# The last 96 FFN columns computed token-major and transposed back by DMA, with the layer norm of the first tile put alone at the front of DVE and ACT

## The chip, the cores and the metric

The kernel runs on one core of one Trainium2 chip. The metric is device time in microseconds (us). "Timed" means runs in rounds of this kernel and the kernel before on the same chip; "the trace" is one profiled execution.

Engines: PE is TensorE (matmul), PEld its weight load, DVE is VectorE, ACT is ScalarE, POOL is GpSimd, SP issues the DMAs. PE's results arrive in the memory called PSUM; `bn_stats` and `bn_aggr` are the DVE instructions for mean and variance. N is the number of columns that a matmul streams, M the number of output partitions.

## The reference

```python
# x: (1, 2048, 512); wqkv: (512, 1536); wo: (512, 512); w1: (512, 1376); w2: (1376, 512); bf16
x = x + A(layernorm(x), wqkv, wo)       # linear attention, 32 heads, phi(t) = where(t>0, t+1, exp(t)) + 1e-6
x = x + B(layernorm(x), w1, w2)         # B: relu(x @ w1) @ w2
x = x + A(layernorm(x), wqkv, wo)
x = x + B(layernorm(x), w1, w2)
```

1376 is ten times 128 plus 96: the last group of FFN columns is not full.

## The kernel before

The kernel writes all instructions into a graph with estimated durations. A list scheduler and a random search then fix the order on each engine. Any edit to the graph makes the search start anew and may move instructions everywhere.

Tokens are handled in 16 tiles of 128, four tiles to a chunk. `Tb` holds the normalized tokens transposed, `xn` untransposed. The first chunk is transposed on PE, the others by DMA from SP. The first half of FFN, in the kernel before (cuts marked):

```python
def b_h(t):
    for c in range(NFC):                       # NFC = 11
        M = 128 if c < NFC - 1 else FLAST      # FLAST = 96
        b = alloc_bank()
        mm_group(... [(psv[0:M, b, :], w1[:, d, 128*c:128*c+M], Tb[:, 4*t:4*t+4, d, :], d == 0, d == 3, False)
                      for d in range(4)] ...)  # 4 matmuls of N=512, also for M=96
        # relu by ACT or DVE into big, columns on partitions
```

The head (first chunk), tile by tile:

```python
def ln_tile_first(i):
    if i in ACT_STATS:     # (2, 3): sum and sum of squares on ACT, small steps on DVE
        ...
    else:                  # tiles 0, 1: bn_stats and bn_aggr on DVE
        ln_stats_first(i)
    # DVE: veps = max(var, 0) + eps;  POOL: rstd = veps ** -0.5;  DVE: nbias = -mean * rstd
    ln_norm(i, True, keys=[("rstd1", i), ("nbias1", i)])   # ACT or DVE
# then, per tile: transpose_pe(i): 4 PE transposes, copied out of PSUM by ACT or DVE
```

Ahead of the head, 12 matmuls on zeros (`WARM=12`) keep PE busy while the first loads arrive.

## Time and profile before

| | before |
|---|---|
| time, median of 6 runs | 289.91 us (289.64 to 290.19) |
| traced execution, span | 288.4 us (it was timed at 290.33) |
| PE busy | 98% |
| start to start of 128x512 matmuls | 216 ns |

The page of the kernel before: busy time of each engine (part 1), and the chain of work that ended last, by engine (part 4).

```profile
PE 282.3 (98%) x1447; PEld 127.9 (44%) x1447; DVE 175.3 (61%) x482; ACT 177.7 (62%) x362; POOL 35.0 (12%) x45
...
PE 90%; DVE 4%; DMA 4%; SPq 0%; issue 0%; ACT 0%
```

PE bounds the kernel, and little else is on the path. "Busy" PE overstates that, because matmuls are pipelined (mean 379 ns each, but one starts every 216 ns). So the holes are read from start times. PE's timeline, before (start, length, engine, line, operation, output and inputs, shape, count, and in brackets the idle time before it with what ended it):

```profile
7.03 1.04 PE L672 MATMUL ps<-wqkv,Tb 128*128 128x512 bf16 x4 [0.69 <-ACT Tb L642]
...
10.61 1.89 PE L672 MATMUL ps<-wqkv,Tb 128*128 128x512 bf16 x8
12.33 1.89 PE L672 MATMUL ps<-Tb,wqkv 128*128 128x512 bf16 x8
...
24.82 1.04 PE L672 MATMUL ps<-wqkv,Tb 128*128 128x512 bf16 x4 [0.24 <-DMA Tb<-xn]
...
45.00 1.06 PE L672 MATMUL ps<-GT,wqkv 128*128 128x128 bf16 x16
...
99.98 9.66 PE L672 MATMUL ps<-Tb,w 128*128 128x512 bf16 x44
...
131.78 6.22 PE L672 MATMUL ps<-Tb,w 128*128 128x512 bf16 x28 [0.54 <-DVE big L852]
...
182.94 1.06 PE L672 MATMUL ps<-GT,wqkv 128*128 128x128 bf16 x16
```

The matmuls `ps<-wqkv,Tb` are the key projections of one tile each, `ps<-Tb,wqkv` the query projections, `ps<-Tb,w` the FFN's first half (44 of them for a chunk, at 99.98 us). The bracket counts idle time after the modelled end of the matmul before; the real loss is the start-to-start time less 216 ns. At 24.82 us (ninth key projection) the gap is 615 ns, so 0.40 us is lost; at 131.78 us it is 918 ns, so 0.70 us is lost. The matmuls on `GT` mark the middle of each attention layer; I use them as milestones, because all the same work lies ahead of them in every kernel here.

The chain of waits, before, in order of time (start, length, what):

```profile
2.23 6.26 DMA xin<-in_A_x_dram
8.50 0.02 issue
8.52 1.29 DVE bst L582 x2
...
19.60 5.17 DMA Tb<-xn
...
24.82 105.58 PE ps L672 x572
```

Until 24.8 us the chain is: second load of x (tiles 4 to 7, landing at 8.50 us; tiles 0 to 3 come ahead of it, in two pieces), work on DVE, then the third DMA transpose of `xn` (tiles 8 and 9). The transpose takes 5.17 us; the page's median for these transposes is 3.2 us.

### The profile page before, as it was taken

What the parts mean: (1) busy time and instruction counts of PE and PEld (TensorE: products, weight loads), DVE (VectorE), ACT (ScalarE), POOL (GpSimd) and SP (SyncE); (2) the same over time, 40 slices, a digit from 0 to 9 for tenths busy, and PEclk for the clock granted to TensorE, in tenths of its full rate; (3) what the DMA queues carried; (4) which work ended last, traced back from release to release, by engine and by line L of the source; (5) the groups of instructions that cost most, each with busy time, mean ns of one, the idle gap of its engine ahead of it and who ended that gap; (6) DMA issues with size and microseconds to landing.
All of it is one profiled execution on the core that took longest, in us unless ns stands there. A gap on an engine that the chain in (4) does not pass through costs nothing.

```text
span 288.4 us, 3983 instructions
## 1 busy us (share of the span) xinstructions
PE 282.3 (98%) x1447; PEld 127.9 (44%) x1447; DVE 175.3 (61%) x482; ACT 177.7 (62%) x362; POOL 35.0 (12%) x45
## 2 busy tenths in 40 slices
PE   7999999999999999999999999999999999999996
PEld 2444454444444444443444444444444444444444
DVE  5899539998358652493345786899854954130233
ACT  5997649999666483586533665999966427316000
POOL 4211000002001110050301373000110011000000
PEclk9999999999999999999999999999999999999999
DMA  7976760213003070030003120012300323001022
GB/s 225 349 101 93 218 211 0 54 22 73 0 2 73 0 146 2 1 73 0 3 0 73 34 41 0 0 35 40 75 2 0 73 71 77 0 32 43 0 73 73
DMA packets 40163, 17.22 MB, mean 60 GB/s; under 512 B 31985, under 2 KB 39633, under 8 KB 40145
## 3 DMA queue, kind: packets, MB, share of 16 engines
q1 hardware_dynamic: 40144, 16.98, 24.8%
q8 instruction: 11, 0.18, 0.3%
q14 instruction: 8, 0.06, 0.1%
HBM read 7.01 MB, written 2.10 MB: 32 GB/s over the span
## 4 chain that ended last, share of the span: by engine, by line
PE 90%; DVE 4%; DMA 4%; SPq 0%; issue 0%; ACT 0%
PE ps L672 90%; DMA xin<-in_A_x_dram 2%; DMA Tb<-xn 2%; DVE bst L582 2%; DVE xn L614 1%; DVE big L658 0%; DVE emscr L656 0%; DVE big L852 0%; DVE mv L583 0%; ACT big L851 0%; DVE xin L870 0%; SPq L539 0%; SPq L534 0%; SPq L536 0%; DVE veps L590 0%
## 5 line engine op out<-in xcount | busy, mean ns | idle before, releaser
L672 PE MATMUL ps<-Tb,w 128*128 128x512 bf16 (+1 forms) x352 | 78.5, 379 | 0.5 <-DVE big L852 0.5
L672 PE MATMUL ps<-w,big 128*128 128x512 bf16 (+2 forms) x363 | 77.3, 372 | 0.0
L851 ACT ACTIVATE big<-ps 128x512 bf16<-128x512 f32 (+1 forms) x79 | 47.0, 601 | 28.2 <-PE ps L672 27.8
L679 ACT ACTIVATE sqscr<-xres 128x512 bf16<-128x512 f32 x48 | 30.0, 626 | 39.3 <-DVE xres L716 25.9
L672 PEld LDWEIGHTS ps<-w,big 128*128 128x128 bf16 (+1 forms) x363 | 35.5, 98 | 40.8
L672 PEld LDWEIGHTS ps<-Tb,w 128*128 128x128 bf16 (+1 forms) x352 | 34.5, 100 | 41.6 <-issue 1.8
L654 ACT ACTIVATE escr<-ps 128x512 bf16<-128x512 f32 x64 | 37.8, 617 | 8.4 <-PE ps L672 8.2
L652 ACT ACTIVATE big<-ps 128x512 bf16<-128x512 f32 x64 | 38.5, 619 | 2.5 <-PE ps L672 2.5
L712 DVE SCALAR_TENSOR_TENSOR xin<-ps,rstdf,xres 128x512 bf16<-128x512 f32 x15 | 11.3, 750 | 37.6 <-PE ps L672 37.5
L672 PE MATMUL ps<-wqkv,Tb 128*128 128x512 bf16 x128 | 31.9, 379 | 1.2 <-ACT Tb L642 0.9
L672 PE MATMUL ps<-big,xn 128*128 128x512 bf16 x128 | 32.2, 379 | 0.0
L658 DVE TENSOR_TENSOR big<-big,emscr 128x512 bf16<-128x512 bf16 x64 | 30.0, 484 | 3.4 <-ACT big L652 2.1
L656 DVE TENSOR_SCALAR emscr<-escr 128x512 bf16<-128x512 bf16 x64 | 21.2, 342 | 14.6 <-ACT escr L654 14.0
L672 PE MATMUL ps<-Tb,wqkv 128*128 128x512 bf16 x128 | 30.0, 379 | 0.0
L672 PE MATMUL ps<-Wp,big 128*128 128x512 bf16 x128 | 29.3, 379 | 0.0
L716 DVE SCALAR_TENSOR_TENSOR xres<-ps,rstdf,xres 128x512 f32<-128x512 f32 x16 | 12.0, 750 | 22.3 <-PE ps L672 22.1
L705 POOL TENSOR_TENSOR rstdf<-varf,nhalf 128x4 f32<-128x4 f32 x8 | 8.3, 1042 | 132.7 <-DVE nm2f L699 75.2
L830 DVE TENSOR_TENSOR big<-big,ps 128x512 bf16<-128x512 bf16 x32 | 20.0, 681 | 3.4 <-PE ps L672 3.4
L672 PEld LDWEIGHTS ps<-wqkv,Tb 128*128 128x128 bf16 x128 | 12.1, 98 | 16.2 <-ACT Tb L642 1.6
L672 PEld LDWEIGHTS ps<-Wp,big 128*128 128x128 bf16 x128 | 12.2, 98 | 15.4 <-DVE Wp L762 0.8
L672 PEld LDWEIGHTS ps<-Tb,wqkv 128*128 128x128 bf16 x128 | 12.2, 98 | 15.0 <-DVE nmf L688 0.5
L672 PEld LDWEIGHTS ps<-big,xn 128*128 128x128 bf16 x128 | 12.2, 98 | 14.6 <-issue 0.5
(89 smaller groups left out, 201.4 us busy)
## 6 DMA issues: line engine op xcount, KB each, us to landing
wqkv<-in_A_wqkv_dram SPq DMA_DIRECT2D x3, 512.0 KB, 7.2
xin<-in_A_x_dram SPq DMA_DIRECT2D x3, 512.0 KB, 8.2
out_dram<-xin SPq DMA_DIRECT2D x3, 512.0 KB, 2.9
w<-in_B_w_dram SPq DMA_DIRECT2D x1, 1376.0 KB, 6.5
w<-in_B_w_dram SPq DMA_DIRECT2D x1, 1280.0 KB, 9.6
wo<-in_A_wo_dram SPq DMA_DIRECT2D x1, 512.0 KB, 8.8
Tb<-xn SPq DMA_TRANSPOSE x30, 3.2
xin<-in_A_x_dram SPq DMA_DIRECT2D x1, 384.0 KB, 3.0
```

The lines of the kernel that those rows point to most:

```text
L582: g.add(DVE, lambda e: e.bn_stats(bst[:, i, :], xin[:, i, :]), [("xin", i)], [("bst", i)], C_DVE_BNST, name="bnst%d" % i)
L652: g.add(ACT, lambda e: e.activation(dst_ap, psv[:, b, :], ACTF.Identity, bias=1.0 + 1e-6, scale=1.0), [("ps", b)], [dst_key], C_ACT_PSUM, ...
L654: g.add(ACT, lambda e: e.activation(escr[:, s, :], psv[:, b, :], ACTF.Exp), [("ps", b)], [("escr", s)], C_ACT_EXP, name=name + "_exp")
L656: g.add(DVE, lambda e: e.tensor_scalar(emscr[:, s, :], escr[:, s, :], 1.0, 1e-6, ALU.min, ALU.add), [("escr", s)], [("emscr", s)], C_DVE_B ...
L658: g.add(DVE, lambda e: e.tensor_tensor(dst_ap, dst_ap, emscr[:, s, :], ALU.max), [dst_key, ("emscr", s)], [dst_key], 340.0, name=name + "_ ...
L672: last = e.matmul(o, l, r, start=st, stop=sp, skip_group_check=skip)
L679: g.add(ACT, lambda e: e.activation(sqscr[:, q, :], xres[:, i, :], ACTF.Square, accum_out=dst[:, i:i + 1]), [("xres", i)], [("sqscr", q), ...
L705: g.add(POOL, lambda e: e.tensor_tensor(rstdf[:, sl], varf[:, sl], nhalf[:, 0:4], ALU.pow), [("varf", t), ("nhalf",)], [("rstdf", t)], C_P ...
L712: g.add(DVE, lambda e: e.scalar_tensor_tensor(xin[:, i, :], psv[:, b, :], rstdf[:, i:i + 1], xres[:, i, :], ALU.mult, ALU.add), rd, [("xin ...
L716: g.add(DVE, lambda e: e.scalar_tensor_tensor(xres[:, i, :], psv[:, b, :], rstdf[:, i:i + 1], xres[:, i, :], ALU.mult, ALU.add, accum_out= ...
L830: g.add(DVE, lambda e, j=j: e.tensor_tensor(unit_ap(us[j]), unit_ap(us[j]), psv[:, GB[j], :], ALU.mult), [("big", us[j]), ("ps", GB[j])], ...
L851: g.add_flex([(ACT, lambda e, M=M, b=b, u=u: e.activation(unit_ap(u, M), psv[0:M, b, :], ACTF.Relu), C_ACT_PSUM), (DVE, lambda e, M=M, b=b ...
```

## The change

The intent, as far as the diff tells it: the 96 columns use 96 of the 128 output partitions, yet cost PE as much as a full group. Computed with tokens as the output partitions, they need N=96 per matmul, so PE streams 16 x 96 columns instead of 4 x 512. The result then has tokens on partitions, so a DMA transpose turns it back. In the head, tile 0 shall be normalized as early as possible: fewer other instructions in front of it, `rstd` by ACT (`Ln`, then `Exp`) for tiles 0 and 1, two warm-up matmuls fewer.

```diff
-... WARM=12, ... SEARCH=1200, ... ACT_STATS=(2, 3)):
+... WARM=10, ... SEARCH=1500, ... ACT_STATS=(2,), REM_TOK=True, RSTD_ACT=(0, 1), FILL=(0,), HEAD_DEP=True):
+        def b_h_rem(t, c, M, b):
+            mm_group(lambda: [(psv[:, b, M*il:M*il+M], Tb[:, 4*t+il, d, :], w1[:, d, 128*c:128*c+M],
+                               d == 0, d == 3, False) for il in range(4) for d in range(4)], ...)
+            # relu of 128 x 4*96 into hrt (ACT or DVE)
+            dma(lambda e: e.dma_start_transpose(unit_ap(u)..., hrt[:, r, :, :]...), ...)
         def b_h(t):
-            for c in range(NFC):
+            for c in ([NFC - 1] + list(range(NFC - 1)) if REM_TOK else range(NFC)):
 ...
-                ln_stats_first(i)
+                ln_stats_first(i, [("xn", i - 1)] if 0 < i < 3 and HEAD_DEP else [])
-            g.add(POOL, ... rstd = veps ** -0.5 ...)      # all tiles
+            if i in RSTD_ACT:                             # tiles 0, 1
+                g.add(ACT, ... lnv = Ln(var + eps) ...); g.add(ACT, ... rstd = Exp(-0.5 * lnv) ...)
-            g.add(DVE, ... nbias = -mean * rstd ...); ln_norm(i, True, ...)        # ACT or DVE
+            g.add(DVE, ... xn = (xin - mean) * rstd ...)                           # DVE alone
```

(`FILL` adds one matmul on zeros behind the transposes of tile 0. POOL also clears `hrt` once.)

More of the change, by code (lines that the diff above doesn't have):

```diff
@@ L24 @@
 C_ACT_SQ = 620.0
+C_ACT_TINY = 220.0
 C_DVE_PSUM = 600.0
@@ L406, in build_kernel @@
 def build_kernel(nc, A_x, A_wqkv, A_wo, B_w1, B_w2, out, n_layers_pairs=2, Q_LATE=3, O_PE_CHUNKS=3, PHI_PATH=3,
-                 KV_LAG=2, INTERLEAVE=True, WARM=12, SPLIT_CHUNKS=1, TAIL_SPLIT=True,
+                 KV_LAG=2, INTERLEAVE=True, WARM=10, SPLIT_CHUNKS=1, TAIL_SPLIT=True,
                  PHI_K=3, PHI_QE=3, PHI_QL=3, LAST_HALVES=True, ZH_FIRST=True, P2_TIGHT=False,
-                 FIRST_PE_CHUNKS=1, TGK=2, TGF=2, FT_PE=0, WP_GB=True, WO_LAG=1, DEN_PRE=1, LATE_A=1, ITERS=12, BOOST=3000.0, SEARCH=1200, ZP=(0, 3), WK_ACT=False, ACT_STATS=(2, 3)):
+                 FIRST_PE_CHUNKS=1, TGK=2, TGF=2, FT_PE=0, WP_GB=True, WO_LAG=1, DEN_PRE=1, LATE_A=1, ITERS=12, BOOST=3000.0, SEARCH=1500, ZP=(0, 3), WK_ACT=False, ACT_STATS=(2,), REM_TOK=True, RSTD_ACT=(0, 1), FILL=(0,), HEAD_DEP=True):
     S = A_x.shape[1]
@@ L474, in build_kernel @@
         zhl = sb("zhl", [128, 2, 512], BF16)
+        hrt = sb("hrt", [128, 2, 4, 128], BF16)
+        eps5 = sb("eps5", [128, 1], F32)
+        lnv = sb("lnv", [128, NT], F32)
         GT = sb("GT", [128, 4, 512], BF16)
@@ L501, in build_kernel @@
         psv = _PS()
-        scr_state = {"e": 0, "sq": 0, "ln": 0}
+        scr_state = {"e": 0, "sq": 0, "ln": 0, "rem": 0}
         def dma(emit, reads, writes, xfer_ns, name, eng=SP, issue=C_SP_ISSUE):
@@ L568, in build_kernel @@
         g.add(POOL, lambda e: e.memset(eps6[:], 1e-6), [], [("eps6",)], 100, name="ms_eps6")
+        g.add(POOL, lambda e: e.memset(eps5[:], EPS), [], [("eps5",)], 100, name="ms_eps5")
         g.add(POOL, lambda e: e.memset(ones[:], 1.0), [], [("ones",)], 200, name="ms_onesb")
@@ L579, in build_kernel, with ln_stats_first @@
               [("m1f",)], [("bmask",)], 300, name="as3")
-        def ln_stats_first(i):
-            g.add(DVE, lambda e: e.bn_stats(bst[:, i, :], xin[:, i, :]), [("xin", i)], [("bst", i)], C_DVE_BNST, name="bnst%d" % i)
+        if REM_TOK:
+            g.add(POOL, lambda e: e.memset(hrt[:], 0.0), [], [("hrt0",), ("hrt", 0), ("hrt", 1)], 400, name="ms_hrt")
+        def ln_stats_first(i, behind=()):
+            g.add(DVE, lambda e: e.bn_stats(bst[:, i, :], xin[:, i, :]), [("xin", i)] + list(behind), [("bst", i)], C_DVE_BNST, name="bnst%d" % i)
             g.add(DVE, lambda e: e.bn_aggr(mv[:, i, :], bst[:, i, :]), [("bst", i)], [("mean", i), ("var", i)], C_DVE_SMALL, name="bnag%d" % i)
@@ L605, in ln_chunk, with ln_norm @@
                   [("mean", i) for i in tl] + [("rstd", t)], [("nbias", t)], C_DVE_SMALL, name="nbias%d" % t)
-        def ln_norm(i, first, eng=None, keys=None):
+        def ln_norm(i, first, eng=None):
             t = i // 4
@@ L610, in ln_norm @@
             skey = ("xin", i) if first else ("xres", i)
-            rd = [skey] + (keys or [("rstd", t), ("nbias", t)])
+            rd = [skey, ("rstd", t), ("nbias", t)]
             alts = [(ACT, lambda e: e.activation(xn[:, i, :], src, ACTF.Identity, scale=rstd[:, i:i + 1], bias=nbias[:, i:i + 1]),
@@ L627, in tr_chunk, with transpose_pe @@
                 tr_dma(lo, lo + grain)
-        def transpose_pe(i):
+        def transpose_pe(i, fill=False):
             b = alloc_bank()
@@ L639, in _emit @@
                 return last
-            g.add(PE, _emit, [("xn", i), ("ident",)], [("ps", b)], 4 * C_MM128, name="trp%d" % i)
+            g.add(PE, _emit, [("xn", i), ("ident",)], [("ps", b)] + ([("fill", i)] if fill else []), 4 * C_MM128, name="trp%d" % i)
+            if fill:
+                g.add(PE, lambda e: e.matmul(psv[:, wt, :], wrm[:, 0:128], wrm[:, :], start=True, stop=True),
+                      [("fill", i)], [("ps", wt)], C_MM512, name="fill%d" % i)
             dst = Tb[:, i, :, :].rearrange("p c t -> p (c t)")
@@ L841, in build_kernel, with src @@
         hcount = [0]
+        def b_h_rem(t, c, M, b):
+            r = scr_state["rem"]
+            scr_state["rem"] = (r + 1) % 2
+            mm_group(lambda: [(psv[:, b, M * il:M * il + M], Tb[:, 4 * t + il, d, :], w1[:, d, 128 * c:128 * c + M],
+                               d == 0, d == 3, False) for il in range(4) for d in range(4)],
+                     [("T", i) for i in range(4 * t, 4 * t + 4)] + [("w1",)], [("ps", b)], 16 * (M / 2.4 + 2.5), "hr%d" % t)
+            def src():
+                return psv[:, b, 0:4 * M].rearrange("p (i m) -> p i m", m=M)
+            g.add_flex([(ACT, lambda e: e.activation(hrt[:, r, :, 0:M], src(), ACTF.Relu), C_ACT_PSUM - 80.0),
+                        (DVE, lambda e: e.tensor_scalar(hrt[:, r, :, 0:M], src(), 0.0, None, ALU.max), C_DVE_FLEX - 120.0)],
+                       [("ps", b), ("hrt0",)], [("hrt", r)], name="hrr%d" % t)
+            u = h_unit(c, t)
+            dma(lambda e: e.dma_start_transpose(unit_ap(u).rearrange("p (i t) -> p i t", t=128),
+                                                hrt[:, r, :, :].rearrange("p i m -> p (i m)")),
+                [("hrt", r)], [("big", u)], 2200.0, "hrt%d" % t, issue=C_SP_TR)
         def b_h(t):
-            for c in range(NFC):
+            for c in ([NFC - 1] + list(range(NFC - 1)) if REM_TOK else range(NFC)):
                 M = 128 if c < NFC - 1 else FLAST
                 b = alloc_bank()
+                if REM_TOK and M < 128:
+                    b_h_rem(t, c, M, b)
+                    continue
                 mm_group(lambda b=b, c=c, M=M: [(psv[0:M, b, :], w1[:, d, 128 * c:128 * c + M], Tb[:, 4 * t:4 * t + 4, d, :],
@@ L911, in ln_tile_first @@
                 g.add(ACT, lambda e: e.activation(sqscr[:, 0, :], xin[:, i, :], ACTF.Identity, accum_out=s1[:, c]),
-                      [("xin", i)], [("sqscr", 0), ("s1", i)], C_ACT_SQ, name="sm%d" % i)
+                      [("xin", i), ("rstd1", 0)], [("sqscr", 0), ("s1", i)], C_ACT_SQ, name="sm%d" % i)
                 g.add(ACT, lambda e: e.activation(sqscr[:, 1, :], xin[:, i, :], ACTF.Square, accum_out=s2[:, c]),
@@ L921, in ln_tile_first @@
             else:
-                ln_stats_first(i)
-            g.add(DVE, lambda e: e.tensor_scalar(veps[:, c], mv[:, i, 1:2], 0.0, EPS, ALU.max, ALU.add),
-                  [("var", i)], [("veps1", i)], C_DVE_SMALL, name="veps%d" % i)
-            g.add(POOL, lambda e: e.tensor_tensor(rstd[:, c], veps[:, c], nhalf[:, 0:1], ALU.pow),
-                  [("veps1", i), ("nhalf",)], [("rstd1", i)], C_POOL_POW1, name="rstd%d" % i)
-            g.add(DVE, lambda e: e.scalar_tensor_tensor(nbias[:, c], mv[:, i, 0:1], -1.0, rstd[:, c], ALU.mult, ALU.mult),
-                  [("mean", i), ("rstd1", i)], [("nbias1", i)], C_DVE_SMALL, name="nbias%d" % i)
-            ln_norm(i, True, keys=[("rstd1", i), ("nbias1", i)])
+                ln_stats_first(i, [("xn", i - 1)] if 0 < i < 3 and HEAD_DEP else [])
+            if i in RSTD_ACT:
+                g.add(ACT, lambda e: e.activation(lnv[:, c], mv[:, i, 1:2], ACTF.Ln, bias=eps5[:, 0:1]),
+                      [("var", i), ("eps5",)], [("lnv", i)], C_ACT_TINY, name="lnv%d" % i)
+                g.add(ACT, lambda e: e.activation(rstd[:, c], lnv[:, c], ACTF.Exp, scale=-0.5),
+                      [("lnv", i)], [("rstd1", i)], C_ACT_TINY, name="rstd%d" % i)
+            else:
+                g.add(DVE, lambda e: e.tensor_scalar(veps[:, c], mv[:, i, 1:2], 0.0, EPS, ALU.max, ALU.add),
+                      [("var", i)], [("veps1", i)], C_DVE_SMALL, name="veps%d" % i)
+                g.add(POOL, lambda e: e.tensor_tensor(rstd[:, c], veps[:, c], nhalf[:, 0:1], ALU.pow),
+                      [("veps1", i), ("nhalf",)], [("rstd1", i)], C_POOL_POW1, name="rstd%d" % i)
+            g.add(DVE, lambda e: e.tensor_scalar(xn[:, i, :], xin[:, i, :], mv[:, i, 0:1], rstd[:, c], ALU.subtract, ALU.mult),
+                  [("xin", i), ("mean", i), ("rstd1", i)], [("xn", i)], C_DVE_NORM_BF, name="norm%d" % i)
         def ln_first(t):
@@ L936, in ln_first @@
                     if t < FIRST_PE_CHUNKS:
-                        transpose_pe(i)
+                        transpose_pe(i, i in FILL)
                     for o in g.ops[n0:]:
```

## The prediction

> **What bounds the kernel now.** TensorE. The page gives PE 98% busy at full clock, but busy time counts pipelined matmuls, so I read start-to-start times: a 128x512 matmul follows the last every 216 ns, and from 10.4 us to the end of the last group (about 285.7 us) only two holes exceed 0.35 us: 0.40 us before the matmuls at 24.82 us (waiting for the third transpose of xn, which took 5.2 us to land instead of the median 3.2) and 0.70 us before those at 131.78 us (waiting for an eviction by DVE). The chain of waits says the same: 90% matmuls. DVE (61%) and ACT (62%) have slack except in the first 25 us, where the chain runs through DVE from the landing of the second x load (8.50 us) to 19.60 us.
>
> **The FFN part.** Eight times, four matmuls of N=512 with M=96 (4 x 216 = 864 ns) become sixteen of N=96 with fresh 128x128 weights each. The sixteen 128x128 matmuls on GT at 45.0 us start every 56 ns, which fits N/2.4 + 2.5 ns in the Trainium skill, "TensorE: Matmul & The Clock Gate", section "Wait — 56ns, not 53.3ns?"; the same page's section "Back-to-back issue gap" would give about 81 ns for N=128 with weight loads, which this trace does not show. The 128x1 matmuls start every 25 ns with new weights, so weights do not bind. Estimate: 16 x 42.6 = 681 ns, a gain of 183 ns per chunk, 1.46 us in all, all on the critical path. The relu eviction shrinks (512 to 384 elements) but is off the path. The eight new DMA transposes cost the queue 1.23 us each and land in about 3.2 us; with the 96-column group first in its chunk, more than 8 us of matmuls lie before their reader. I expect no wait for them.
>
> **The head.** Two warm-up matmuls fewer frees PE at 5.48 us instead of 5.96. rstd of tile 0 goes through two small ACT instructions instead of POOL, but the instruction order puts a 0.63 us Square (waiting for the load that lands at 4.22) between them, and on DVE a bn_stats, aggregate and eps lie before the normalization. I expect tile 0 normalized at about 5.7 us (before: 5.44), transposed at 5.8 (before 5.96), first projection at 6.8 (before 7.03). That lead is not kept: DVE's order has bn_stats of tile 4, whose data lands at 8.50 us, ahead of the normalizations of tiles 1 and 2. DVE will idle about 1.2 us, tile 1 is normalized at about 9.5 us, and the fourth projection ends near 12.9 us, against 12.33. Part returns at the 24.2 us wait, which should shrink. Net estimate: +0.2 us (-0.3 to +0.6).
>
> **The wait at 131 us.** The schedule was searched anew; there ACT now evicts more of the FFN groups. I count half of the 0.7 us as gone: -0.3.
>
> **Sum.** 289.81 - 1.46 + 0.2 - 0.3 = 288.25 us; 8 in 10 between 287.4 and 289.3. Chances: faster by over 2%: 0.01; within 2%: 0.98; slower: 0.01.
>
> **What would show it.** Starts of the N=96 matmuls every 42 to 44 ns; no wait of PE for big written by the new transposes; DVE idle until about 8.5 us before a bn_stats, with tile 1 normalized after it; the first query projection starting at 12.6 to 13.0 us; first projection before 7.0 us.
>
> **What would make it wrong.** N=96 matmuls bound at 56 ns or above (no gain in the FFN); the new transposes delaying those of xn behind them in the one queue; new holes in PE where the new order meets evictions; a clock that rises later because of the shorter warm-up; the x load landing elsewhere than at 8.5 us.

## The result

| | before | changed |
|---|---|---|
| time, median of 6 runs | 289.91 us (289.64 to 290.19) | 289.26 us (288.99 to 289.65) |
| ratio | | 0.9978 (0.9965 to 0.9991) |
| traced execution, span | 288.4 us | 287.3 us |

A ratio is the mean time of one kernel's fast runs over that of the other's of the same rounds, so it is not quite the ratio of the medians. The median lies inside the predicted range, but the gain is 0.65 us where I predicted 1.56 us.

The page of the changed kernel, the same parts as before:

```profile
PE 280.5 (98%) x1542; PEld 129.5 (45%) x1542; DVE 176.0 (61%) x478; ACT 174.4 (61%) x359; POOL 34.8 (12%) x45
...
PE 94%; DMA 4%; DVE 1%; SPq 0%; ACT 0%; issue 0%
```

PE's timeline, changed, the lines that answer to those of before (and the new ones of N=96):

```profile
7.21 1.04 PE L683 MATMUL ps<-wqkv,Tb 128*128 128x512 bf16 x4 [0.47 <-ACT Tb L653]
...
9.62 0.40 PE L646 MATMUL ps<-ident,xn 128*128 128x128 bf16 x4 [1.16 <-DVE xn L964]
...
12.78 3.62 PE L683 MATMUL ps<-Tb,wqkv 128*128 128x512 bf16 x16
...
25.77 1.04 PE L683 MATMUL ps<-wqkv,Tb 128*128 128x512 bf16 x4 [0.74 <-DMA Tb<-xn]
...
45.95 1.06 PE L683 MATMUL ps<-GT,wqkv 128*128 128x128 bf16 x16
...
100.57 0.84 PE L683 MATMUL ps<-w,Tb 128*128 128x96 bf16 x16
101.25 8.80 PE L683 MATMUL ps<-Tb,w 128*128 128x512 bf16 x40
...
128.71 8.97 PE L683 MATMUL ps<-Tb,w 128*128 128x512 bf16 x40
...
182.63 1.06 PE L683 MATMUL ps<-GT,wqkv 128*128 128x128 bf16 x16
```

The sixteen matmuls of N=96 take 101.25 - 100.57 = 0.68 us; their starts lie 42.5 ns apart. The hole at 131 us is nearly gone: its group starts 380 ns after the last, so 0.17 us is lost instead of 0.70. The hole before the ninth key projection has grown: the gap is 1122 ns, so 0.90 us is lost instead of 0.40. The matmuls on `GT` start 0.95 us later.

The chain of waits, changed: again load, DVE, third transpose.

```profile
2.23 6.30 DMA xin<-in_A_x_dram
8.54 0.02 issue
8.56 0.69 DVE bst L590
...
20.49 5.24 DMA Tb<-xn
...
25.77 106.56 PE ps L683 x628
```

The third transpose takes 5.24 us again, but is issued at 20.49 us instead of 19.60. DVE's timeline, changed, shows what was put where:

```profile
7.53 0.15 DVE L960 TENSOR_SCALAR veps<-mv 128x1 f32<-128x1 f32 x1
8.56 0.69 DVE L590 BATCH_NORM_STATS2 bst<-xin 128x6 f32<-128x512 bf16 x1 [0.88 <-DMA xin<-in_A_x_dram]
9.17 0.40 DVE L964 TENSOR_SCALAR xn<-xin,mv,rstd 128x512 bf16<-128x512 bf16 x1
9.48 0.42 DVE L654 COPY Tb<-ps 128x512 bf16<-128x512 bf16 x1
9.82 0.41 DVE L964 TENSOR_SCALAR xn<-xin,mv,rstd 128x512 bf16<-128x512 bf16 x1
```

DVE idles 0.88 us for the load of tile 4. Behind it stand the normalization of tile 1 (9.17 us), the copy of tile 3 (9.48) and the normalization of tile 2 (9.82), none of which needs that load. The `rstd` of tile 1 was ready at 7.7 us. In the kernel before, DVE normalized tile 1 (or 2) at 6.70 us, and only one tile of the head stood behind the load. DVE's timeline, before:

```profile
8.52 1.29 DVE L582 BATCH_NORM_STATS2 bst<-xin 128x6 f32<-128x512 bf16 x2 [0.56 <-DMA xin<-in_A_x_dram]
...
9.90 0.41 DVE L614 TENSOR_SCALAR xn<-xin,rstd,nbias 128x512 bf16<-128x512 bf16 x1
```

The new buffer `hrt`, in the view of one tile's instructions:

```profile
L863 ACT ACTIVATE hrt<-ps x8: 469/491/586, 62.0 to 257.0; 128x384 bf16<-128x384 f32 x8
...
who waited for it (us, times):
busy tenths in 40 slices 1000000000000000000000000000000000000000
DMA to landing us min/median/max: 2.4/2.8/4.2
```

The list of who waited is empty, and the new transposes land in 2.8 us.

**The sum by stages.** Span cut at the starts of the two groups on `GT`; all from traces. The second x load lands at a different time in each execution (8.11 to 9.21 us), and in most kernels here the head shifts with it, so I also give the head counted from that landing.

| kernel (trace) | x load lands | to first GT | from the landing | first GT to second | second GT to end |
|---|---|---|---|---|---|
| before | 8.50 | 45.00 | 36.50 | 137.94 | 105.41 |
| r_before (same kernel) | 8.81 | 44.90 | 36.09 | 137.94 | 105.42 |
| changed | 8.54 | 45.95 | 37.41 | 136.68 | 104.65 |
| r_after (same kernel) | 8.31 | 45.62 | 37.31 | 136.67 | 104.67 |
| a_ffn | 8.18 | 44.27 | 36.09 | 136.72 | 104.95 |
| r_ffn (same kernel) | 8.56 | 44.69 | 36.13 | 136.72 | 104.94 |
| b_head | 8.93 | 46.04 | 37.11 | 137.47 | 105.41 |
| d2_order | 9.09 | 44.83 | 35.74 | 136.68 | 104.67 |
| r_d2 (same kernel) | 8.82 | 44.88 | 36.06 | 136.67 | 104.67 |

From GT to the end, four 96-column groups became shorter: -0.76 us. Between the two GT there are four more, and the 131 us hole: -1.26 us, of which -0.53 is the hole. So the FFN groups gave about 1.49 us and the hole 0.53. The head took back 0.9 to 1.3 us counted from the landing.

### The profile page after: what moved, and what is told of

The parts are those of the page before. It is cut to its first block, busy times and chain, and to the rows that moved or that the text cites. A ratio compares the mean times of both kernels' runs of the same rounds, so it can differ in the third digit from the quotient of the medians.

```text
span 287.3 us, 4176 instructions
## 1 busy us (share of the span) xinstructions
PE 280.5 (98%) x1542; PEld 129.5 (45%) x1542; DVE 176.0 (61%) x478; ACT 174.4 (61%) x359; POOL 34.8 (12%) x45
## 4 chain that ended last, share of the span: by engine, by line
PE 94%; DMA 4%; DVE 1%; SPq 0%; ACT 0%; issue 0%
PE ps L683 93%; DMA xin<-in_A_x_dram 2%; DMA Tb<-xn 2%; DVE bst L590 0%; PE ps L646 0%; ACT escr L665 0%; DVE xin L901 0%; SPq L543 0%; SPq L538 0%; SPq L540 0%; DVE xn L964 0%
## 5 line engine op out<-in xcount | busy, mean ns | idle before, releaser
L683 PE MATMUL ps<-Tb,w 128*128 128x512 bf16 x320 | 71.6, 379 | 0.0
L882 ACT ACTIVATE big<-ps 128x512 bf16<-128x512 f32 x69 | 41.0, 599 | 16.8 <-PE ps L683 16.4
L683 PEld LDWEIGHTS ps<-Tb,w 128*128 128x128 bf16 x320 | 30.5, 98 | 36.3 <-issue 0.9
L663 ACT ACTIVATE big<-ps 128x512 bf16<-128x512 f32 x64 | 38.2, 614 | 2.6 <-PE ps L683 2.6
```

Of the source, the lines that this page charges most:

```text
L663: g.add(ACT, lambda e: e.activation(dst_ap, psv[:, b, :], ACTF.Identity, bias=1.0 + 1e-6, scale=1.0), [("ps", b)], [dst_key], C_ACT_PSUM, ...
L683: last = e.matmul(o, l, r, start=st, stop=sp, skip_group_check=skip)
L882: g.add_flex([(ACT, lambda e, M=M, b=b, u=u: e.activation(unit_ap(u, M), psv[0:M, b, :], ACTF.Relu), C_ACT_PSUM), (DVE, lambda e, M=M, b=b ...
```

## The experiments

Two theories of the head's loss: (T1) the **order on DVE**, which puts ready work behind the load; (T2) the **instruction fetch of PE**. The packets in the trace show instructions being fetched by DMA in blocks of 16 KB on one queue. That these are PE's is inferred from their number: 11 before and 12 in the changed kernel, where PE has 2,926 and 3,123 instructions in the trace. In these two kernels one such fetch comes after 82 to 84 matmuls, at 20.43 us (before) and 21.56 us (changed), while the third transpose is in flight, and that transpose is the slow one. A rival to both: the head is neutral, and the FFN part lost its gain in new waits.

### c_fetch: the fetch moved by the warm-up's shape (orders kept)

```diff
-                for k in range(WARM):
-                    last = e.matmul(psv[:, wt, :], wrm[:, 0:128], wrm[:, :], start=True, stop=True)
+                for k in range(60):
+                    last = e.matmul(psv[:, wt, 0:80], wrm[:, 0:128], wrm[:, 0:80], start=True, stop=True)
```

> The changed kernel, with its warm-up as 60 matmuls of N=80 in place of 10 of N=512: every engine's order is otherwise the same. In both traces TensorE's 16 KB instruction fetch comes after 82 to 84 matmuls, at 20.4 us (before) and 21.6 us (changed), in the middle of the third transpose of xn, which then takes 5.2 us instead of 3.1. Theory (the fetch delays that transpose, and this is the lost part of the gain): with 50 more matmuls ahead, the fetch comes at about 11 to 13 us, the third transpose lands in 3.0 to 3.5 us, TensorE's 0.9 us hole at 24.9 us closes to under 0.1 us, and the time falls by about 0.9 us against the changed kernel, to about 288.3 us. Rival (the third transpose is slow for another reason, such as the load of the queue or of SBUF at that time): it still takes about 5.2 us, the hole stays, time 289.2 us.

Measured: 288.78 us median (287.51 to 291.27), ratio 0.9971 (0.9934 to 1.0008). The fetch came at 14.62 us, the third transpose was issued at 20.84 us and landed at 23.90, after 3.06 us, and the hole was gone. PE's timeline of c_fetch:

```profile
7.17 1.89 PE L683 MATMUL ps<-wqkv,Tb 128*128 128x512 bf16 x4 [0.69 <-ACT Tb L653]
...
25.23 1.03 PE L683 MATMUL ps<-wqkv,Tb 128*128 128x512 bf16 x4
```

But the first key projection took 1.89 us instead of 1.04 (first line), while the ninth started without a wait (last line): the granted clock rose to full only at 10.7 us (5.5 us in the changed kernel). Two of the six runs had mean clocks of 0.988 and 0.994 and took 291.1 and 291.3 us. So the run agrees with T2 about the transpose; its time is inconclusive.

### d_bn4: one instruction moved behind the normalization of tile 1 (rest kept)

```diff
         order, total = _list_schedule(...)
+        # in order[DVE]: take "bnst4" out, put it back right after "norm1"
```

> The changed kernel with one DVE instruction moved after scheduling: bn_stats of tile 4 (whose data lands at 8.5 us) goes behind the normalization of tile 1, nothing else. Theory A (the head is late because DVE's order holds tile 1 behind that load, and the first matmuls bound everything after): tile 1 is normalized at about 8.2 us instead of 9.6, the first query projection starts 0.3 us earlier (12.4 to 12.5 us), and the time falls by 0.3 us. Theory B (what counts is the third transpose with its delay by the instruction fetch, released by DVE's whole work after 8.5 us): DVE has one 0.33 us normalization less after 8.5 us, so the third transpose may start 0.3 us earlier, but the fetch also comes 0.3 us earlier; the hole at 24.9 us keeps about its 0.9 us. Both say 288.9 to 289.0 us; they differ in the hole: 0.9 us if it moves with the rest, 1.2 us (and no gain at all) if the transpose does not move.

Measured: 288.90 us, ratio 0.9965 (0.9951 to 0.9980). In its trace tile 1 was normalized at 7.57 us, but the next instruction behind the load was now the copy of tile 3, which PE needed first: the next key projection did not start before 10.31 us, with the load landing at 9.21 us. The hole before the ninth key projection was 0.92 us, the third transpose took 5.26 us. So the wait moved to the next victim. The run does not tell the two theories apart as I had hoped; it showed that the whole group has to move.

### a_ffn: the FFN part alone, with the old head (schedule searched anew)

```diff
 (kernel before)
+        hrt = sb("hrt", [128, 2, 4, 128], BF16)      # with its clearing by POOL, b_h_rem and the new loop in b_h
```

> The kernel before with the FFN part of the change alone (old head, 12 warm-up matmuls, old search length; the schedule is searched anew). Theory (FFN part worth 1.46 us, head part negative): each 16 matmuls of N=96 take 0.68 us, no wait of TensorE for the new transposes, head as before (fifth to eighth projections as before, hole at 24.2 us about 0.4 us), hole at 131 us anywhere in 0 to 0.7 us: time 287.9 to 288.5 us, faster than the full change. Rival (the FFN part loses some of its gain in new waits and the head is neutral): about 289.2 us.

Measured: 288.34 us, ratio 0.9948 (0.9918 to 0.9977). By the median it is faster than the full change, but one of its six runs (290.88 us at a mean clock of 0.992) widens the interval until it overlaps that of the change; r_ffn below settles it. No wait for the new transposes.

### b_head: the head part alone (schedule searched anew)

```diff
 (changed kernel)
-... REM_TOK=True, ...
+... REM_TOK=False, ...
```

> The changed kernel with the FFN part undone (96-row groups as before), new head kept, schedule searched anew. Theory (the head part costs about 0.9 us): about 290.3 to 290.9 us, slower than before, with the hole before the ninth key projection at 0.5 us or more. Rival (head neutral): 289.7 to 290.0 us.

Measured: 290.67 us, ratio 1.0022 (1.0003 to 1.0042): slower than before by 0.64 us, although its hole at 131 us shrank to 0.18 us too. That shrinking therefore comes from the search and not from the FFN part. Counted from the landing, its head is 0.6 to 1.0 us longer than before. The hole before the ninth projection was only 0.12 us, not the 0.5 that I expected: this schedule lost its time earlier, its first query projection starting at 13.53 us. The rival "FFN part lost its gain" falls with these two runs.

### c2_pad and f2_before_pad: the fetch moved by satisfied waits (orders kept)

```diff
                     last = e.matmul(psv[:, wt, :], wrm[:, 0:128], wrm[:, :], start=True, stop=True)
+                    for _w in range(10):
+                        e.wait_ge(sem_eng[DVE], 1)
```

> The changed kernel with ten already satisfied waits after each of its ten warm-up matmuls: 100 more instructions for TensorE to fetch, no other work, same orders, and (other than in c_fetch) the warm-up matmuls as they were, so the clock should rise at about 5.4 us again. Theory (TensorE's instruction fetch delays the third transpose of xn): the 16 KB fetch comes before 17 us instead of at 21.6, the third transpose takes 3.0 to 3.5 us instead of 5.2, TensorE's 0.9 us hole before the ninth key projection is under 0.1 us, the matmuls on GT start at about 45.05 us instead of 45.95, and the time is 0.9 us below the changed kernel: 288.2 to 288.6 us. Rival (the transpose is slow for another reason; c_fetch moved it by its changed clock): hole and time as in the changed kernel, 289.2 us.

Measured: 289.96 us, ratio 0.9987 (0.9963 to 1.0011). The waits were not free: warm-up matmuls started about 550 ns apart instead of 427, so the transposes of tile 0 began at 6.96 us instead of 6.12. And the fetch did not come before 17 us, but at 19.49, into the **second** transpose. That one now took 4.57 us, and the third took 3.06. PE's timeline of c2_pad has the hole at the seventh key projection:

```profile
20.48 1.03 PE L685 MATMUL ps<-big,xn 128*128 128x512 bf16 x4
22.10 1.04 PE L685 MATMUL ps<-wqkv,Tb 128*128 128x512 bf16 x4 [0.59 <-DMA Tb<-xn]
```

The hole followed the fetch from the third transpose to the second. The time says nothing, as the head was delayed otherwise.

> The kernel before with the same padding (120 more waits behind its 12 warm-up matmuls). Theory: its third transpose of xn lands in 3.0 to 3.5 us instead of 5.2, the 0.4 us hole before 24.8 us closes, the time falls by 0.4 us to about 289.5 us. Rival: no change, 290.0 us.

Measured: 291.50 us, ratio 1.0051 (1.0029 to 1.0074), slower: the first key projection started at 9.06 us instead of 7.03. The hole before the ninth projection was gone, but with PE that late it would be gone anyway. Its third transpose took 3.69 us, although no 16 KB fetch fell into it (that came at 15.87 us); a fetch of 8 KB on another queue did, at 22.74 us. A miss: the padding cost more than what it was to measure.

### d2_order: the whole group in front of the load (rest kept)

```diff
         order, total = _list_schedule(...)
+        # in order[DVE], the eight from "bnst4" to "trev2" become:
+        want = ["norm1", "trev3", "norm2", "bnst4", "bnst5", "trev2", "bnag4", "bnst6"]
```

(`norm` is a normalization, `trev` the copy of a transposed tile out of PSUM, `bnst` bn_stats, `bnag` its aggregate.)

> The changed kernel with eight DVE instructions reordered after scheduling: normalization of tile 1, the copy of the transposed tile 3, the normalization of tile 2 come ahead of the bn_stats of tile 4 (data at 8.2 to 9.2 us), and bn_stats of tiles 4 and 5 ahead of the copy of tile 2; nothing else moves. Theory: the first four key projections end about 1.0 us earlier and the first query projection starts at 11.7 to 12.0 us instead of 12.8; but the fetch still falls on the third transpose, so the hole before the ninth key projection grows to about 1 to 1.5 us, and the matmuls on GT start only 0.3 to 0.7 us earlier: 288.6 to 289.0 us. Rival (order of DVE in the head is what costs, the fetch is a bystander): the whole 1.0 us arrives at the end, 288.2 us.

Measured: 287.87 us (287.59 to 288.29), ratio 0.9923 (0.9903 to 0.9943): 1.3 us faster than the changed kernel, with the same work and the same order on all other engines. DVE's timeline of d2_order, to be held against that of the changed kernel:

```profile
7.72 0.41 DVE L964 TENSOR_SCALAR xn<-xin,mv,rstd 128x512 bf16<-128x512 bf16 x1
8.62 0.42 DVE L654 COPY Tb<-ps 128x512 bf16<-128x512 bf16 x1 [0.49 <-PE ps L646]
8.96 0.40 DVE L964 TENSOR_SCALAR xn<-xin,mv,rstd 128x512 bf16<-128x512 bf16 x1
9.28 1.28 DVE L590 BATCH_NORM_STATS2 bst<-xin 128x6 f32<-128x512 bf16 x2
```

PE's timeline of d2_order:

```profile
9.11 1.04 PE L683 MATMUL ps<-wqkv,Tb 128*128 128x512 bf16 x4 [0.30 <-DVE Tb L654]
11.93 3.62 PE L683 MATMUL ps<-Tb,wqkv 128*128 128x512 bf16 x16
...
24.66 1.04 PE L683 MATMUL ps<-wqkv,Tb 128*128 128x512 bf16 x4
...
44.83 1.06 PE L683 MATMUL ps<-GT,wqkv 128*128 128x128 bf16 x16
```

Both normalizations now stand ahead of the bn_stats of tile 4 (9.28 us), and DVE doesn't wait for the load any more. The first query projection starts at 11.93 us instead of 12.78, although the load landed 0.55 us later here (9.09 us). The third transpose was issued at 20.23 us and took 4.38 us; the gap before the ninth key projection is 356 ns, so 0.14 us is lost. A new hole of 0.45 us (gap 670 ns) stands at 17.60 us, where PE waits for DVE. T1 holds: eight instructions of DVE in another order are worth about 1.3 us. The number was a miss, below both what the theory and what the rival had said.

The gain came at the query projections: counted from the landing they start 1.40 us earlier than in the changed kernel. The hole that was expected to grow did not, because the transpose took 4.38 us and not 5.24; its margin (defined below) even shrank. PE's holes behind the first query projection add up to 0.59 us here and to 0.90 us in the changed kernel.

### e2_both: the order of d2_order and the padding of c2_pad

```diff
 (d2_order)
                     last = e.matmul(psv[:, wt, :], wrm[:, 0:128], wrm[:, :], start=True, stop=True)
+                    for _w in range(10):
+                        e.wait_ge(sem_eng[DVE], 1)
```

> c2_pad and d2_order together. Theory: both waits gone, the matmuls on GT start 1.3 to 1.9 us earlier than in the changed kernel (44.0 to 44.6 us), time 287.4 to 288.0 us: below the kernel before, the changed kernel and each of the two alone. If only one of the two causes is real, it equals the better of the two alone.

Measured: 288.71 us (288.44 to 289.08), ratio 0.9951 (0.9931 to 0.9971). A miss: slower than d2_order alone by 0.84 us. The fetch came at 20.34 us, ahead of the third transpose, which then took 3.04 us (21.13 to 24.17), and the hole before the ninth projection was gone. But the padding made PE begin the transposes of tile 0 at 6.96 us and the first key projection at 8.23, and that cost more than the hole of 0.14 us that was left to win. So moving the fetch by waits does not pay, and the runs with padding cannot price the fetch.

### r_after, r_d2 and r_ffn: the three kernels again, on one chip

No edit: the changed kernel, d2_order and a_ffn, in shared rounds, so that they can be compared with one another.

> The changed kernel again, unchanged, on the same chip as the two beside it: 289.0 to 289.5 us, with the matmuls on GT at 45.5 to 46.3 us and the hole before the ninth key projection near 0.9 us if the reading of its first trace is right in general and not of one execution.

Measured: 289.29 us (289.05 to 289.83), ratio 0.9973 (0.9958 to 0.9987).

> d2_order again: 287.6 to 288.1 us, 1.1 to 1.5 us below the changed kernel of the same rounds. If its first result came from a chip or from where the x loads landed, it would be within 0.5 us of it.

Measured: 288.02 us (287.67 to 288.32), ratio 0.9926 (0.9910 to 0.9941).

> a_ffn again: 287.8 to 288.5 us. If d2_order's head is better than the old head, it is 0.3 us or more above r_d2; otherwise the two are equal, which would say that the new head, once ordered well, is worth nothing over the old one.

Measured: 287.95 us (287.80 to 288.37), ratio 0.9927 (0.9913 to 0.9941).

The gain of the changed kernel repeats (0.27%), and so do the larger ones of d2_order and a_ffn (0.73 to 0.74%). The last two are equal within their spread: the new head, in a good order, is worth nothing over the old head. As the change was delivered, its head costs 289.29 - 287.95 = 1.34 us, with the reserve that a_ffn has another schedule behind the head too. In the trace of r_after the hole before the ninth projection is there again (gap 1019 ns, 0.80 us lost), after a third transpose of 5.15 us issued at 20.25 us. In the trace of r_d2, PE loses 0.45 us at 17.43 us and 0.36 us before the ninth projection (gap 572 ns), after a third transpose of 4.60 us: as much in all as in r_after. Its first query projection starts 2.94 us after the landing (r_after 4.24), and that difference of 1.30 us is the whole gain. d2_order and a_ffn both beat both kernels.

### r_before: a second trace of the kernel before

> The kernel before again, for a second trace of it. Its first traced execution (290.33 us) was slower than its timed median (289.9). If the first trace is typical, the third transpose of xn again takes over 4 us with TensorE's 16 KB fetch inside it, the hole before the ninth key projection is 0.2 to 0.5 us, the 0.7 us wait at 131 us is there again, and the matmuls on GT start at 44.6 to 45.1 us. If the 131 us wait is absent, the share of the gain that I gave to it belongs elsewhere.

Measured: 290.29 us in a single look (the kernel before beside it: 289.72). The hole of 0.70 us at 131 us is there again (gap 919 ns). The hole before the ninth key projection is not, as PE's timeline of r_before shows:

```profile
24.73 1.03 PE L672 MATMUL ps<-wqkv,Tb 128*128 128x512 bf16 x4
26.46 1.03 PE L672 MATMUL ps<-wqkv,Tb 128*128 128x512 bf16 x4
```

The third transpose took 3.62 us (19.92 to 23.54), although the fetch of 16 KB (at 20.82 us, 0.97 us long) fell into it. Hence the hole of 0.40 us in the first trace of before is not in every execution, and a fetch in flight does not always stretch the transpose to 5 us. Both traced executions of before ran about 0.4 us slower than its median, so a difference of two traced spans (288.4 - 287.3 = 1.1 us) overstates the gain; the timed runs decide.

## Why the prediction was right or wrong

| part | predicted | measured | from |
|---|---|---|---|
| FFN groups | -1.46 us | -0.76 - (1.26 - 0.53) = -1.49 us | the stage table |
| hole at 131 us | -0.30 us | 0.17 - 0.70 = -0.53 us | the gaps at 131 us |
| head | +0.20 us | +0.9 to +1.3 us | stage table, from the landing; r_after - r_ffn gives 1.34 |
| sum | -1.56 us | -0.65 us (r_after: 0.75 below the kernel before of its rounds) | timed medians |

**The FFN part: right, in mechanism and size.** The matmuls of N=96 start every 42.5 ns, with fresh weights each (predicted 42 to 44). No instruction of PE waited for the new transposes. a_ffn, with this part alone, has the same two stages to 0.05 and 0.3 us; the 0.3 us lies behind the last matmul (3.23 us from its start to the end of the span, 2.94 in the changed kernel), so it is not PE's.

**The hole at 131 us: right in kind, a little too small.** b_head, without the FFN part, lost only 0.18 us there too, so the new search closed it, as I had supposed, and not the new groups. The size was a guess, and that more evictions by ACT closed it was not tested.

**DVE waiting for the load: right.** DVE idled until the landing (8.54 us), the normalizations of tiles 1 and 2 came behind it, and the first query projection started at 12.78 us (predicted 12.6 to 13.0). Counted from the landing it started 4.25 us (r_after 4.24) after it, before 3.84 (r_before 3.84): 0.41 us later, where I had reckoned with about half a microsecond. Three small points were off: DVE idled 0.88 us and not 1.2; tile 0 was normalized at 6.07 us and not 5.7, as the load of tiles 1 to 3 landed 0.40 us later than in the trace of before, and the first projection started at 7.21 us and not before 7.0.

**The step that failed** is the head's net: "Net estimate: +0.2 us (-0.3 to +0.6)", and within it "Part returns at the 24.2 us wait, which should shrink." That wait grew, from 0.40 us lost to 0.90 (r_after 0.80). I let the delay end at the first query projection and took the transpose of 5.2 us for an accident of one trace. I did not follow DVE's extra work behind the load to the next thing it releases, the third transpose. The traces have this sum:

| | before | changed | d2_order | a_ffn |
|---|---|---|---|---|
| third transpose issued, after the landing of x | 11.11 us | 11.95 us | 11.14 us | 10.47 us |
| first query projection, after the landing of x | 3.84 us | 4.25 us | 2.84 us | 3.84 us |
| from that to where PE wants the transpose (12.09 us later), less its issue: the margin | 4.82 us | 4.39 us | 3.80 us | 5.47 us |
| the transpose took | 5.17 us | 5.24 us | 4.38 us | 4.37 us |
| lost before the ninth key projection | 0.40 us (r_before 0) | 0.90 us (r_after 0.80) | 0.14 us (r_d2 0.36) | 0 |

(The 12.09 us are 24.42 - 12.33 in before, where 24.42 is the start of the ninth key projection, 24.82, less the 0.40 us lost. About 0.05 us pass from landing to start, which is why latency less margin falls short of the loss by that. d2_order has a hole of 0.45 us in between, so its margin is 4.25 us in fact.)

The transpose was issued 0.84 us later after the landing, because DVE had more work behind it. By its timelines there were two copies out of PSUM (0.33 us each from start to start) and one bn_stats (0.60 us) more than before, and one normalization (0.33 us) less: one more of the head, but two fewer of the later tiles, which the new schedule gave to ACT. PE itself got there only 0.41 us later. So the margin shrank by 0.43 us while the latency stayed at 5.2 us, and the hole grew by about as much. By these sums the delay of DVE was paid twice: 0.41 us at the query projection and 0.4 to 0.5 us more at the transpose. Together that is 0.9 us, the traced loss of the head. The second payment needs the slow transpose too: at the 3.62 us of r_before, a margin of 4.39 us would have left no hole.

What is shown by experiment is that DVE's order costs: with nothing but that order changed, d2_order starts the query projections 1.40 us and issues the transpose 0.81 us earlier after the landing, and is 1.3 us faster. It does not price the two payments apart. PE comes earlier too, so the margin did not recover (3.80 us), and the holes behind the query projections stayed (0.59 us against 0.90; in r_d2 and r_after 0.81 against 0.80). The second payment is therefore a sum from the traces, not shown by a run of its own. The rest up to 1.3 us is the luck of the one trace of before, in which PE lost 0.40 us that it does not always lose.

**What stays open.** Whether the fetch of PE's instructions costs time by itself. Third transposes without a 16 KB fetch in them took 3.04 to 3.06 us (c_fetch, c2_pad, e2_both) and 3.69 us (f2_before_pad), those with one 3.62 us (r_before), 4.3 to 4.6 us (a_ffn, r_ffn, d2_order, r_d2) and 5.04 to 5.26 us (before, changed, r_after, d_bn4, b_head), and in c2_pad the slow transpose went where the fetch went.

The 14 traces hold 500 DMA transposes. Of the 343 with no instruction fetch of 8 or 16 KB in flight between issue and landing, none took more than 3.48 us; of the 157 with one, 87 took more than 3.5 us, up to 5.29. A transpose's packets mostly take 0.02 us each. In the third transposes of over 5 us, and in r_d2's of 4.60, two groups of packets stood for 0.5 to 1.8 us each, one during or just after the 16 KB fetch, the other just after a fetch of 8 KB (queue q14; whose instructions those are the trace does not say). In a_ffn, r_ffn, r_before and d2_order (3.62 to 4.38 us) there was one such group. So what differs between 3.6 and 5.2 us is the number and length of these stalls. The DMA view of before, for the 5.2 us of its third transpose, shows the rate in 40 slices of 0.13 us, with the two stalls at about 21.6 to 22.7 and 23.1 to 23.9 us, and the two fetches (packets, MB, share of the DMA engines' time):

```profile
GB/s 0 0 0 0 0 0 126 0 0 126 215 270 195 146 55 6 0 0 4 8 10 8 10 10 77 264 77 8 8 8 6 8 10 228 286 267 291 291 291 286
...
q14 instruction: 1, 0.01, 2.2%
q8 instruction: 1, 0.02, 1.9%
```

That is close agreement and still not an experiment. No run moved the fetch alone: c_fetch changed the clock, c2_pad, f2_before_pad and e2_both delayed the head. Open too is how much of a_ffn's lead is a luckier search.

The Trainium skill, "Runtime: NRT & Kernel Launch", section "Instruction fetch mechanics", says that instructions are refilled in blocks of 16 KiB and calls the cost of crossing a boundary "mostly hidden". The traces agree with the block for PE: transfers of 16 KB, the first of them after 81 to 84 matmuls in every kernel with the usual warm-up and no padding (99 in c_fetch). Other instructions came in blocks of 8 KB. PE itself was never seen to stop for one; what the traces add is the company of slow transposes.

## What to carry to other kernels

On an engine whose instructions start in their order, as DVE's did here, ready work belongs ahead of an instruction that waits for a load: eight instructions in another order were worth about 1.3 us here, nearly as much as the whole rewrite of the FFN group (1.49 us). When a delay is costed, follow it past its first victim to the next transfer that it issues, and compare that transfer's margin with the latency that it has shown, not with its median; count such times from the landing of the load, which itself moved by a microsecond between executions. And where a search fixes the order, test an edit with all other orders kept, because a new search changes everything else with it.

## What the Trainium skill lacked or had wrong

- "TensorE: Matmul & The Clock Gate", section "Back-to-back issue gap": about 81 ns at N=128 and 131 ns at N=512 for streams of weight load and matmul. The runs show 56 ns (N=128), 42.5 ns (N=96) and 216 ns (N=512), with weights loaded for each. The formula N/2.4 + 2.5 ns of the same page fits all three.
- The same page, section "What's actually happening", the table of clock states: full clock after at least one busy window of about 3.4 us. The runs with the usual warm-up, which began at 1.24 us, had it between 3.94 us (d_bn4) and 6.85 us (r_ffn). In c_fetch sixty warm-up matmuls of N=80, 4.0 us without a pause, were followed by full clock only at 10.7 us. That need not contradict the page, whose windows are not aligned to the kernel's start, but how busy a window must be it does not say (only that PE transposes do not count in the same way).
- "Runtime: NRT & Kernel Launch", section "Instruction fetch mechanics": nothing of other transfers. With an instruction fetch in flight 87 of 157 DMA transposes took more than 3.5 us, up to 5.29; without one none of 343 took more than 3.48 us. That the fetch is the cause is not proved.
- No page has the cost of a wait on PE that is already satisfied: ten of them between cold matmuls stretched the spacing from 427 to about 550 ns, by estimate some 12 ns a wait.
- No page says how far the landing of a load varies: the second load of x landed between 8.11 and 9.21 us, from one execution to the next and between kernels that issue it alike.
